# Splitting the first weight loads, moving part of a projection into the start, and reading a few short rows early, in a sliding-window attention kernel

## The chip, the cores and the metric

One core of a Trainium2 chip. The metric is the device time of one execution in microseconds (us), as the median of several executions. "Span" is the time from the first to the last instruction of the program as the profile shows it, and is shorter than the time by what lies outside it. All comparisons of times below are between executions in the fast state; one profiled execution (of e6) fell in the slow one, and is marked. A ratio is the mean time of one kernel's fast runs over that of the other's of the same rounds, so it is not quite the ratio of the medians quoted beside it. In the profile's lines `<-` before a name in brackets gives what an engine waited for, and a "trace" is the record of the one execution of a kernel that was profiled.

Engines are named as in the profile: PE does matmuls, PEld is its weight loads, DVE is VectorE, ACT ScalarE, POOL GpSimd, SP the engine that issues most loads.

## The reference

```python
# B=8, Sq=32, D=1024, Hq=32, Hkv=4, Sk=8192, Dh=128; all bfloat16
W = min(4096, max(256, Sk // 4))                       # 2048: only the last W keys and values
q = (x @ wq).reshape(B, Sq, Hq, Dh).transpose(0, 2, 1, 3)
k = jnp.repeat(k_cache[:, :, Sk - W:, :], rep, axis=1)  # rep = 8 query heads share one K/V head
v = jnp.repeat(v_cache[:, :, Sk - W:, :], rep, axis=1)
p = softmax(einsum("bhqd,bhkd->bhqk", q, k) * Dh ** -0.5)
out = einsum("bhqk,bhkd->bhqd", p, v).transpose(0, 2, 1, 3).reshape(B, Sq, Hq * Dh) @ wo
```

There are 32 pairs of a batch and a K/V head. The kernel calls each a unit; it has 2048 keys, 512 KB of K and 512 KB of V.

## The kernel before

The kernel runs the units one after another. A unit has four slots. In each slot PE makes scores for 512 keys, ACT takes their exp, and PE multiplies the exps of two slots ago with V. All other PE work (the q projection of the next group of heads, the output projection, turning K of the next unit) is hung on the slots as "pieces".

The start has no slots. It loads x and the first group's part of wq (eight chunks of 256 KB), turns x with PE, makes q of group 0, and turns K of unit 0:

```python
Q_CUT = 4
N_WARM = (7, 0, 0)

    def start(self):
        wz = self.c1.tile([P, 512], BF16, name="wz")
        nc.vector.memset(wz[:, :], 0.0)
        nc.sync.dma_start(out=x_sb[:, 0, :], in_=xf[0:P, :])
        nc.scalar.dma_start(out=x_sb[:, 1, :], in_=xf[P:2 * P, :])
        wq0 = self.load_wq(0, 0, (1, 1, 2)) + self.load_wq(0, 1, (2, 1, 1))   # chunks 0 | 1 | 2,3 | 4,5 | 6 | 7
        for p in wq0[:4]:
            p()
        self.load_k(0, 0)                    # first half of K of unit 0
        wq0[4]()
        wq0[5]()
        self.load_k(0, 1)                    # second half
        self.load_v(0, nc.sync)
        self.load_k(1)
        self.load_v(1, nc.sync)
        # ... weights of later groups are collected in self.weights
        for ui in range(2, 4):
            self.load_unit(ui)               # K and V of units 2 and 3, K of 5, two pieces of wq of group 1
        # ... memsets
        warm_up(N_WARM[0])                   # 7 matmuls of 512 columns on wz, to keep PE busy until x is there
        # ... turn x
        for c in range(self.DC):             # 8 chunks
            for h in range(self.rep):        # 8 heads
                q_mm(c, h, 0, P if c >= Q_CUT else self.NQ)      # from chunk Q_CUT on only the first 128 rows of q
            if c == self.DC - 3:
                k_turn(0); k_copy(0)         # first half of K0
        k_turn(1)                            # second half of K0
        # ... copy q of batch 0; k_copy(1); va_copy(0)
        def q_rest(k):                       # the other 128 rows, chunks Q_CUT to 7: two of these in slot 0, two in slot 1
            for h in (2 * k, 2 * k + 1):
                for c in range(Q_CUT, self.DC):
                    q_mm(c, h, P, self.NQ)
            q_copy("v", k, 1, self.B)
```

All loads but one go through SP's queue, in program order. The order after the start is set by these lines:

```python
V_T = {5: (2, (5, 6, 8, 10), 10, 17, 12), **{u: (u - 4, ...) for u in (8, 11, ...)}}  # K of these units is turned by DVE and GpSimd
W_AT = (3, 3, 4, 4, 8, 8, ...)               # after which unit's loads each piece of wq or wo is loaded

    def load_unit(self, ui):
        # K, V of the unit, then K of a V_T unit that is due, then weight pieces with W_AT == ui
    def k_pieces(self, ui):                  # PE turns K of unit 1 to 4, in the four slots of the unit before (unit 1: in the last two)
    Q_SLOTS = {1: (17, 31), ...}             # q of group 1 is made in slots 17 to 30
```

## Time and profile before

| | |
|---|---|
| time, median of 3 runs | 186.94 us (186.40 to 186.98); of 6 runs 186.74 |
| span of the profiled execution | 184.6 us |
| PE busy | 97% |
| first exp starts | 14.02 us |

These lines are from the page of the kernel before. After the span comes the busy time of each engine; then, in 40 slices of the span, the busy tenths of PE and what the DMA engines moved; the count of instruction fetches in part 3; and the shares of the chain of work that ended last.

```profile
span 184.6 us, 5089 instructions
...
PE 179.9 (97%) x2072; PEld 153.7 (83%) x2072; DVE 115.2 (62%) x267; ACT 131.8 (71%) x133; POOL 94.7 (51%) x150
...
GB/s 159 297 396 408 402 398 396 238 206 228 384 361 255 369 274 314 403 267 221 354 341 246 358 391 235 281 278 384 258 314 399 233 264 321 188 240 28 4 30 91
...
q8 instruction: 16, 0.26, 0.6%
...
PE 93%; DMA 4%; SPq 1%; DVE 1%; issue 0%
```

The table of waits, PE's lines only: who waited for whom, total us, times, the longest.

```profile
PE warm_ps L347 <- DVE wz L316: 1.2, 1, 1.2
...
PEld L377 <- DMA wq_sb<-in_wq_dram: 1.2, 2, 1.0
PEld L356 <- DMA x_sb<-in_x_dram: 0.8, 1, 0.8
PE q_ps L377 <- DMA wq_sb<-in_wq_dram: 0.7, 1, 0.7
...
PEld L370 <- DMA k_raw<-in_k_cache_dram: 0.2, 1, 0.2
```

PE waits for weights of q (L377), for x, and a little for K0's second half (L370).

The chain that ended last, in order of time, its first 18 us (start, us, what; short pieces are left out):

```profile
2.12 6.54 DMA wq_sb<-in_wq_dram
...
8.70 2.81 PE q_ps L377 x32
...
12.92 0.62 PE kf_ps L370 x8
13.54 0.44 PE s_ps L469 x4
13.98 0.89 PE q_ps L377 x16
```

Chunks 2 and 3 arrive as one load at 8.65 us; PE had finished chunk 1 at about 7.8. At 12.92 it starts to turn K0's second half, makes the first scores, and then the second half of the q matmuls (L377 x16 is 0.89 us) inside slot 0.

### The profile page before, as it was taken

To read this page: it belongs to the slowest core of one execution; us is meant where nothing else is said; L and a number is where in the kernel's file an instruction comes from. 1 tells how busy PE (TensorE), PEld (TensorE's weight loads), DVE (VectorE), ACT (ScalarE), POOL (GpSimd) and SP (SyncE) were. 2 spreads that over 40 slices of the span, in tenths; PEclk is the share of its full clock that TensorE was granted. 3 is DMA by queue.
4 is the path that set the end of the run, shared out by engine and by line. 5 is a ranking of instruction groups with operands and counts; after the bars stand their busy time and mean duration, and the time that the engine had idled before them with its cause. 6 is when DMAs were issued, how large, how long until landed. Compare 5 with 4: busy or idle time off the path is not lost.

```text
span 184.6 us, 5089 instructions
## 1 busy us (share of the span) xinstructions
PE 179.9 (97%) x2072; PEld 153.7 (83%) x2072; DVE 115.2 (62%) x267; ACT 131.8 (71%) x133; POOL 94.7 (51%) x150
## 2 busy tenths in 40 slices
PE   7899999999999999999999999999999999999994
PEld 2799999999999999987788899988787888888843
DVE  0238799994586686586467648656755865265363
ACT  2207899787789777777878677887877888888800
POOL 2000007949939959928954990797199379700000
PEclk9999999999999999999999999999999999999999
DMA  6999999999999989999999999999999999891003
GB/s 159 297 396 408 402 398 396 238 206 228 384 361 255 369 274 314 403 267 221 354 341 246 358 391 235 281 278 384 258 314 399 233 264 321 188 240 28 4 30 91
DMA packets 53082, 51.73 MB, mean 280 GB/s; under 512 B 39744, under 2 KB 40256, under 8 KB 53056
## 3 DMA queue, kind: packets, MB, share of 16 engines
q1 hardware_dynamic: 52480, 50.90, 98.9%
q10 hardware_dynamic: 576, 0.49, 0.8%
q8 instruction: 16, 0.26, 0.6%
q14 instruction: 10, 0.08, 0.2%
HBM read 41.42 MB, written 0.52 MB: 227 GB/s over the span
## 4 chain that ended last, share of the span: by engine, by line
PE 93%; DMA 4%; SPq 1%; DVE 1%; issue 0%
PE o_ps L480 31%; PE s_ps L469 30%; PE op_ps L295 15%; PE q_ps L275 11%; DMA wq_sb<-in_wq_dram 4%; PE q_ps L377 2%; PE tp L236 2%; PE kf_ps L370 1%; SPq L164 0%; DVE kT L374 0%; SPq L321 0%; DVE o_t L305 0%; DVE QT_63 L397 0%; PE cnt_ps L534 0%
## 5 line engine op out<-in xcount | busy, mean ns | idle before, releaser
L471 ACT ACTIVATE pT<-s_ps 128x1024 bf16<-128x1024 f32 x128 | 128.9, 1025 | 33.3 <-PE s_ps L469 32.3
L261 POOL TENSOR_SCALAR kTv<-kb 32x512 bf16<-32x512 bf16 x140 | 93.7, 670 | 65.1 <-PE s_ps L469 38.6
L480 PEld LDWEIGHTS <-pT 128*128 128x128 bf16 x1024 | 68.4, 98 | 3.2
L469 PEld LDWEIGHTS <-kT 128*128 128x128 bf16 x368 | 34.7, 98 | 10.4
L295 PE MATMUL op_ps<-wo_sb,OT 128*128 128x512 bf16 (+2 forms) x144 | 36.2, 356 | 0.0
L275 PE MATMUL q_ps<-xT,wq_sb 128*128 128x256 bf16 x192 | 28.1, 273 | 0.0
L480 PE MATMUL o_ps<-va_112,pT 128*128 128x129 bf16 x352 | 27.2, 220 | 0.0
L480 PE MATMUL o_ps<-va_113,pT 128*128 128x129 bf16 x352 | 27.0, 220 | 0.0
L480 PE MATMUL o_ps<-va_114,pT 128*128 128x129 bf16 x320 | 24.7, 220 | 0.0
L251 DVE STREAM_TRANSPOSE kb<-k_raw 128x512 bf16<-128x512 bf16 x36 | 23.8, 684 | 0.0
L417 DVE RECIPROCAL RL_all<-o_ps 128x2 f32<-128x2 f32 x32 | 5.3, 164 | 27.5 <-PE o_ps L480 27.5
L422 DVE TENSOR_SCALAR o_sb<-o_ps,RL_all 128x128 bf16<-128x128 f32 x64 | 19.5, 346 | 1.1
L469 PEld LDWEIGHTS <-kTv 128*128 128x128 bf16 x144 | 13.9, 98 | 5.1
L275 PEld LDWEIGHTS <-wq_sb 128*128 128x128 bf16 x192 | 17.0, 98 | 1.2
L469 PE MATMUL s_ps<-QT_63,kT 128*128 128x256 bf16 x112 | 16.8, 273 | 0.0
L424 DVE STREAM_TRANSPOSE OT<-o_sb 128x256 bf16<-128x256 bf16 x32 | 14.2, 445 | 1.1
L469 PE MATMUL s_ps<-QT_66,kT 128*128 128x256 bf16 x96 | 14.4, 273 | 0.0
L295 PEld LDWEIGHTS <-OT 128*128 128x128 bf16 x144 | 11.4, 98 | 2.3 <-DVE OT L424 0.2
L469 PE MATMUL s_ps<-QT_65,kT 128*128 128x256 bf16 x80 | 12.0, 273 | 0.0
L469 PE MATMUL s_ps<-QT_64,kT 128*128 128x256 bf16 x80 | 12.0, 272 | 0.0
L302 DVE TENSOR_TENSOR oacc<-op_ps,oacc 128x512 f32<-128x512 f32 x8 | 5.5, 682 | 7.4 <-PE op_ps L295 7.4
L411 DVE COPY va_113<-v_sb 128x2048 bf16<-128x2048 bf16 x11 | 9.5, 860 | 0.0
(45 smaller groups left out, 105.1 us busy)
## 6 DMA issues: line engine op xcount, KB each, us to landing
v_sb<-in_v_cache_dram SPq DMA_DIRECT2D x29, 512.0 KB, 6.9
wo_sb<-in_wo_dram SPq DMA_DIRECT2D x16, 512.0 KB, 6.8
wq_sb<-in_wq_dram SPq DMA_DIRECT2D x14, 512.0 KB, 6.9
k_raw<-in_k_cache_dram SPq DMA_DIRECT2D x13, 512.0 KB, 6.3
v_sb<-in_v_cache_dram SPq DMA_DIRECT2D x6, 256.0 KB, 6.5
wq_sb<-in_wq_dram SPq DMA_DIRECT2D x4, 256.0 KB, 6.4
kT<-in_k_cache_dram SPq DMA_TRANSPOSE x36, 6.8
k_raw<-in_k_cache_dram SPq DMA_DIRECT2D x2, 256.0 KB, 7.9
```

The source lines that it names most:

```text
L251: nc.vector.transpose(out=st["kb"][:, sl, :], in_=self.k_raw[ui][:, sl, :])
L261: nc.gpsimd.tensor_scalar(out=out, in0=in_, scalar1=1.0, scalar2=1.0, op0=ALU.mult, op1=ALU.mult)
L275: nc.tensor.matmul(st["ps"][:, 0:self.NQ], lhsT=self.wq_t[g, i][:, c % (DC // 2), hl * P:(hl + 1) * P], rhs=self.xT[:, c, :], start=(c == ...
L295: nc.tensor.matmul(ps[:, 0:w], lhsT=self.OT[:, gq, c, t * P:(t + 1) * P], rhs=self.wo_t[gq][:, c, n0:n0 + w], start=(k == 0), stop=(k == 7))
L302: nc.vector.tensor_tensor(out=acc, in0=ps[:, 0:w], in1=acc, op=ALU.add)
L411: self.nc.vector.tensor_copy(out=self.va[ui % 3][:, :, 0:self.Dh], in_=self.v_sb[ui][:, :, :])
L417: nc.vector.reciprocal(out=rl[:, ui * QT_N:(ui + 1) * QT_N], in_=o_ps[:, :, Dh])
L422: nc.vector.tensor_scalar(out=o_sb[:, qt, :, :], in0=o_ps[:, qt, 0:Dh].rearrange("p (i c) -> p c i", c=4), scalar1=rl[:, ui * QT_N + qt:ui ...
L424: nc.vector.transpose(out=self.OT[:, g * QT_N:(g + 1) * QT_N, :, b * self.Sq:(b + 1) * self.Sq], in_=o_sb[:, :, :, :])
L469: nc.tensor.matmul(s_ps[:, jj, :], lhsT=self.kT[ui][:, c * CJ + jj, :], rhs=q_u, start=True, stop=True)
L471: nc.scalar.activation(out=pT[:, :, :], in_=s_ps[:, :, :], func=ACT.Exp, bias=0.0, scale=self.scale)
L480: nc.tensor.matmul(o_ps[:, qt, 0:self.VW], lhsT=pT[:, jj, qt * P:(qt + 1) * P], rhs=va[:, j, 0:self.VW], start=(j == 0 and qt == 0), stop= ...
```

## The change

The intent is to shorten the start. Chunks 2 and 3 come as two loads. Chunks 4 and 5 get all their rows at once (`Q_CUT` 6), so that less is left for slots 0 and 1. The warm-up reads a constant that exists before the start, so PE need not wait for DVE. GpSimd's queue reads 16 short rows each of wq, K and V first, to take a possible cost of first access off the big loads. The V load of unit 29 is no longer cut in two.

```diff
-Q_CUT = 4
-N_WARM = (7, 0, 0)
+Q_CUT = 6
+N_WARM = (8, 0, 0)
-V_HALVES = 29
+V_HALVES = 30
@@ start
-        wz = self.c1.tile([P, 512], BF16, name="wz")
-        nc.vector.memset(wz[:, :], 0.0)
+        one = nc.const_aps.tensor
-        wq0 = self.load_wq(0, 0, (1, 1, 2)) + self.load_wq(0, 1, (2, 1, 1))
-        for p in wq0[:4]:
+        wq0 = self.load_wq(0, 0, (1, 1, 1, 1)) + self.load_wq(0, 1, (2, 1, 1))
+        for p in wq0[:5]:
             p()
         self.load_k(0, 0)
-        wq0[4]()
         wq0[5]()
+        wq0[6]()
@@
+        first = self.c1.tile([16, 3, 32], BF16, name="first")
+        for i, src in enumerate((self.wq[0:16, 0:32], self.k_cache[0, 0, self.Sk - self.W:self.Sk - self.W + 16, 0:32],
+                                 self.v_cache[0, 0, self.Sk - self.W:self.Sk - self.W + 16, 0:32])):
+            nc.gpsimd.dma_start(out=first[:, i, :], in_=src)
@@ warm_up
-                nc.tensor.matmul(warm[:, :], lhsT=wz[:, 0:P], rhs=wz[:, :], start=True, stop=True)
+                nc.tensor.matmul(warm[:, :], lhsT=one(1.0, [P, P], BF16), rhs=one(1.0, [P, 512], BF16), start=True, stop=True)
```

## The prediction

> **What bounds it now.** The page gives PE 97% busy; the chain of waits is 93% PE, 4% DMA. Its only DMA piece is the load of wq chunks 2 and 3: issued at 2.12 us, released PE at 8.70. The table of waits gives PE four real waits: warm-up on the zeroed tile (until 1.20 us), x (0.8 us, to 4.30), wq (0.7-1.0 us, to 8.70), the second K half (0.2 us, to 12.92). From the first scores (13.38 us) to the end PE runs on its own work. So the change can win only in the first 13 us, or by emptying the slots after.
>
> **What the change does, costed.**
> 1. Loads split. x lands about 4.3, chunk 0 at 6.03, chunk 1 at 6.72, chunks 2+3 together at 8.65, 4+5 at 10.0. A chunk is 8 matmuls 0.109 us apart: 0.87 us. PE runs out near 7.83. Chunk 2 alone should land near 7.7 (half of the pair's 1.93 us), so the 0.7-1.0 us wait almost closes. The extra issue (0.47 us of SP) is hidden: the stream limits, not the issuing.
> 2. Q_CUT 4 to 6 moves 16 matmuls of 128 columns (0.055 us each, 0.88 us) from the first two score slots into the start. No work disappears; it fills point 1's hole. Slots 0 and 1 shrink from 1.33 to 0.90 us each.
> 3. Warm-up: the constant of ones is written before the start barrier, so PE starts near 0.85 instead of 1.20, eight matmuls at 0.427 us end near 4.27. That spacing is the cold clock of the Trainium skill, "TensorE: Matmul & The Clock Gate", Part 1 (half rate until about 3.4 us of activity); the trace agrees: x's transposes start 0.107 us apart until about 5.7 us, then 0.055. Starting sooner may warm PE sooner: worth 0 to 0.3 us.
> 4. Short GpSimd reads. DMA moves about 400 GB/s at 3-4 us and after 10 us, but 236-303 at 4-7 and 272-293 at 8-10, when wq and K are first read, some packets taking 0.4 to 1.15 us, not 0.084. At about 400 GB/s the loss is about 1.4 us of landing time. The first packets of x took 0.7 us too. The reads should pay such a cost early. But V's first reads show no such dip, so I give it 45%. They may also slow x.
> 5. Unit 29's V in one load: nothing.
>
> **Sum.** Without help from 4: chunks 0-3 run 6.08-9.56, wait for 4+5 (10.0), 10.05-11.79, K half 12.24, chunks 6, 7 13.12, second K half 13.57: first scores 0.2 us later, 0.88 us less afterwards: net -0.7. With help: PE never waits after 6.0, first scores at about 13.1: net -1.15; earlier warmth up to -0.4 more. All on the critical path.
>
> **Predicted: 185.9 us** (186.94 before, -0.6%), eight times in ten 185.0 to 186.9. Faster by over 2%: 3%; within 2%: 95%; slower: 2%.
>
> **Signs.** Warm-up before 0.9 us; no q matmul wait near 7.8-8.7, perhaps one at chunk 4; first scores 13.0-13.6; slots 0, 1 0.9 us apart; DMA at 4-7 and 8-10 us near 400 GB/s if 4 works, unchanged if not; unit 1 on unchanged.
>
> **What would make it wrong.** x landing later because the short reads stall the engines; identity late behind the short reads; DVE copies of q becoming a wait in slots 2 and 3 (they follow V's landing, 14.15 us); the gain lost to ScalarE (1.02 us per slot against 0.90).

## More of the kernel before

PE is the bound: it is busy nearly always and the last-ending chain is 93% PE. But slices 3 to 7 (9 to 32 us, 4.6 us each) move about 400 GB/s without a break; no later stretch of that length moves as much (one single slice has 403).

## The result, and the profile after

The changed kernel takes 186.70 us (median of 6 runs, 186.08 to 187.09) against 186.74 before (6 runs). The ratio is 0.9996, with a 95% interval of 0.9972 to 1.0021: the same. The predicted gain of 0.6% is not there. 186.70 lies inside the predicted range of 185.0 to 186.9 all the same, but so does the 186.74 of the unchanged kernel: that the time fell in the range says nothing for the mechanism.

The answering lines of the page:

```profile
span 184.5 us, 5062 instructions
...
PE 180.8 (98%) x2057; PEld 154.1 (83%) x2057; DVE 115.6 (63%) x266; ACT 131.6 (71%) x133; POOL 96.3 (52%) x153
...
GB/s 155 341 369 414 405 401 391 223 184 360 283 346 257 357 243 357 401 269 241 370 361 246 364 392 233 242 327 384 261 362 345 227 260 287 216 219 0 0 33 88
...
q8 instruction: 15, 0.25, 0.5%
...
PE 83%; DMA 14%; SPq 1%; issue 0%; DVE 0%
```

The span is the same to 0.1 us, with 15 fewer matmuls. But the share of DMA in the chain went from 4% to 14%. The chain in order of time shows where:

```profile
2.59 5.97 DMA wq_sb<-in_wq_dram
...
8.58 9.36 DMA v_sb<-in_v_cache_dram
...
17.96 10.40 DMA k_raw<-in_k_cache_dram
```

The chain no longer follows PE through the first units. It follows loads up to 17.96 + 10.40 = 28.36 us, when K of unit 4 lands. Before that moment nothing that PE saved counts. The waits agree:

```profile
PEld L359 <- DMA x_sb<-in_x_dram: 0.9, 1, 0.9
PE warm_ps L350 <- PEq L645: 0.8, 1, 0.8
PEld L236 <- DMA k_raw<-in_k_cache_dram: 0.5, 2, 0.3
...
PEld L380 <- DMA wq_sb<-in_wq_dram: 0.2, 1, 0.2
...
PEld L373 <- DMA k_raw<-in_k_cache_dram: 0.2, 1, 0.2
```

The wait for chunks 2 and 3 is gone, as intended; the 0.2 us left on a load of wq (L380) is for chunks 4 and 5, which landed at 9.86 us. In its place PE waits twice for K of a later unit (L236, the turning of K). Here is the first of the two places, before and after, in PE's weight loads in order of time; and below it the second.

Before:

```profile
19.55 0.27 PEld L236 LDWEIGHTS <-k_raw 128*128 128x128 bf16 x4
...
28.45 0.27 PEld L236 LDWEIGHTS <-k_raw 128*128 128x128 bf16 x4
```

After:

```profile
19.26 0.23 PEld L236 LDWEIGHTS <-k_raw 128*128 128x128 bf16 x4 [0.26 <-DMA k_raw<-in_k_cache_dram]
...
28.41 0.23 PEld L236 LDWEIGHTS <-k_raw 128*128 128x128 bf16 x4 [0.24 <-DMA k_raw<-in_k_cache_dram]
```

The trace's issue and semaphore records give the landings. "Lead" is how much earlier an exp starts than the same exp of the kernel before.

| | K0, second half | first exp | K2 lands | K4 lands | lead at exp 4 | at exp 5 | at exp 13 | at the last exp |
|---|---|---|---|---|---|---|---|---|
| before | 12.88 | 14.02 | 19.29 | 28.40 | | | | |
| after | 13.13 | 14.27 | 19.22 | 28.37 | 0.58 | 0.32 | 0.08 | 0.09 |

The start won 0.58 us, and two waits took 0.26 and 0.24 of it. The sums close. Before, PE turned K2 0.26 us after it had landed (19.55 less 19.29); K2 now lands 0.07 us earlier; so PE can lead there by 0.33 at most, and 0.32 is measured. For K4 it is 0.05 + 0.03 = 0.08, and 0.08 to 0.09 is measured. Put shortly: the lead can be no more than 19.55 less the landing of K2, and then no more than 28.45 less the landing of K4.

How the 0.58 came about is seen in ACT's exps in order of time (start, busy us), before:

```profile
14.02 1.02 ACT L471 ACTIVATE pT<-s_ps 128x1024 bf16<-128x1024 f32 x1 [1.00 <-PE s_ps L469]
15.35 1.02 ACT L471 ACTIVATE pT<-s_ps 128x1024 bf16<-128x1024 f32 x1 [0.31 <-PE s_ps L469]
16.68 1.02 ACT L471 ACTIVATE pT<-s_ps 128x1024 bf16<-128x1024 f32 x1 [0.31 <-PE s_ps L469]
18.01 1.02 ACT L471 ACTIVATE pT<-s_ps 128x1024 bf16<-128x1024 f32 x1 [0.31 <-PE s_ps L469]
```

and after:

```profile
14.27 2.88 ACT L474 ACTIVATE pT<-s_ps 128x1024 bf16<-128x1024 f32 x3 [0.96 <-PE s_ps L472]
17.43 1.02 ACT L474 ACTIVATE pT<-s_ps 128x1024 bf16<-128x1024 f32 x1 [0.28 <-PE s_ps L472]
18.77 1.02 ACT L474 ACTIVATE pT<-s_ps 128x1024 bf16<-128x1024 f32 x1 [0.31 <-PE s_ps L472]
20.20 1.02 ACT L474 ACTIVATE pT<-s_ps 128x1024 bf16<-128x1024 f32 x1 [0.41 <-PE s_ps L472]
```

Exps are counted from 0. Exp 0 is 0.25 us later (14.27 against 14.02). Exps 0 to 2 then follow almost without a gap instead of every 1.33 us, so exp 3 (17.43 against 18.01) and exp 4 (18.77 against 19.35) are 0.58 us ahead. The last line shows the lead being lost: from exp 4 to exp 5 (18.77 to 20.20) it takes 1.43 us, where the kernel before took 1.18 (19.35 to 20.53).

Last, the stretches of the start for the kernel before. Columns: the stretch, its length, busy us of PE, PEld, DVE, ACT, POOL (with instructions), granted clock, DMA share, GB/s.

```profile
4.00:8.00 4.00, 3.97 (x33) 2.98 (x32) 0.92 (x3) 1.17 (x2) 0.00 (x0) 1.00 0.98 299
8.00:10.00 2.00, 1.30 (x12) 1.18 (x13) 0.00 (x0) 0.00 (x0) 0.00 (x0) 1.00 1.01 283
10.00:12.00 2.00, 2.00 (x34) 1.94 (x33) 0.01 (x1) 0.00 (x0) 0.00 (x0) 1.00 1.05 406
12.00:16.00 4.00, 3.95 (x64) 3.66 (x62) 3.55 (x8) 2.10 (x4) 0.00 (x0) 1.00 1.03 415
```

and after:

```profile
4.00:8.00 4.00, 4.00 (x33) 3.33 (x33) 0.92 (x3) 1.17 (x2) 0.00 (x0) 1.00 0.92 300
8.00:10.00 2.00, 2.00 (x20) 1.62 (x18) 0.00 (x0) 0.00 (x0) 0.00 (x0) 1.00 1.04 384
10.00:12.00 2.00, 2.00 (x23) 1.82 (x22) 0.00 (x0) 0.00 (x0) 0.00 (x0) 1.00 1.01 313
12.00:16.00 4.00, 3.99 (x59) 3.66 (x57) 3.29 (x7) 2.16 (x4) 0.00 (x0) 1.00 1.03 417
```

The dip at 8 to 10 us moved to 10 to 12; it did not go. By 13 us the loads are where they were, or 0.25 us behind.

### The profile page after: what moved, and what is told of

Read it like the earlier page. It is cut to its first block, busy times and chain, and to the rows that moved or that the text cites. A ratio compares the mean times of both kernels' runs of the same rounds, so it can differ in the third digit from the quotient of the medians.

```text
span 184.5 us, 5062 instructions
## 1 busy us (share of the span) xinstructions
PE 180.8 (98%) x2057; PEld 154.1 (83%) x2057; DVE 115.6 (63%) x266; ACT 131.6 (71%) x133; POOL 96.3 (52%) x153
## 4 chain that ended last, share of the span: by engine, by line
PE 83%; DMA 14%; SPq 1%; issue 0%; DVE 0%
PE o_ps L483 29%; PE s_ps L472 27%; PE op_ps L295 15%; PE q_ps L275 11%; DMA k_raw<-in_k_cache_dram 6%; DMA v_sb<-in_v_cache_dram 5%; DMA wq_sb<-in_wq_dram 3%; SPq L164 1%; PE tp L236 1%; SPq L320 0%; DVE o_t L305 0%; PE cnt_ps L537 0%
```

## The experiments

Theory A: from about 9 to 33 us the loads run at their full rate, 1.28 us for 512 KB, and K2 and K4 landed just in time before. A start that is faster on PE meets loads that are not faster, and hands the lead back. Theory B, a rival: the lead went with the phase of PE's clock. In the trace's records of the granted clock, full speed came at 5.69 us before and 6.57 us after (PE's transposes of x start 0.107 us apart until 5.6 us before and 0.055 apart from 5.7; the clock column of the stretches above shows 1.00 throughout and is no guide here). Before, PE's hole near 8 us may have hidden such a delay. Rival C: the order of the loads alone matters, not the start. A last question was whether the short reads do anything.

Twelve kernels were run, all correct, each in five timed rounds and a profile. The table has what the traces and rounds gave; the texts after it say what each was for. "Over" counts executions whose time exceeds their span by more than 2.0 us.

| kernel | Q_CUT | K0's second half lands | full clock from | lead at exp 4 | at exp 16 | at the last | ratio to before (95%) | mean span, it / before | over |
|---|---|---|---|---|---|---|---|---|---|
| changed | 6 | 13.13 | 6.57 | 0.58 | 0.09 | 0.09 | 0.9996 (0.9972 to 1.0021) | 184.58 / - | 2 of 6 |
| e1_k4_first | 6 | 13.05 | 5.26 | 0.65 | 0.57 | -0.01 | 1.0039 (1.0001 to 1.0077) | 185.00 / 184.67 | 3 of 6 |
| e2_k2_k4_first | 6 | 12.87 | 6.23 | 0.83 | 0.83 | 0.65 | 0.9994 (0.9975 to 1.0013) | 184.48 / 184.67 | 1 of 6 |
| e3_before_k2_k4 | 4 | 13.16 | 7.16 | -0.28 | -0.28 | -0.28 | 1.0034 (1.0001 to 1.0066) | 185.25 / 184.67 | 0 of 6 |
| e5_before_k4_late | 4 | 13.19 | 4.66 | -0.32 | -1.29 | -1.29 | 1.0054 (1.0032 to 1.0076) | 185.70 / 184.67 | 0 of 6 |
| e6_deadline_order | 6 | 14.10 | 3.92 | -0.39 | -0.39 | -0.68 | 1.0019 (0.9986 to 1.0051) | 184.92 / 184.65 | 1 of 6 |
| e7_before_deadline | 4 | 13.40 | 5.16 | -0.52 | -0.52 | -0.81 | 1.0022 (1.0006 to 1.0038) | 185.15 / 184.65 | 0 of 6 |
| e8_deadline_no_reads | 6 | 12.90 | 4.48 | 0.80 | 0.81 | 0.51 | 1.0006 (0.9987 to 1.0025) | 184.60 / 184.65 | 1 of 6 |
| e9_deadline_qcut4 | 4 | 12.97 | 3.86 | -0.09 | -0.09 | -0.39 | 1.0018 (1.0005 to 1.0032) | 185.05 / 184.65 | 0 of 6 |
| e10_deadline_fixed | 6 | 12.98 | 6.10 | 0.71 | 0.71 | 0.30 | 1.0025 (0.9993 to 1.0056) | 184.42 / 184.55 | 3 of 6 |
| e11_fixed_no_reads | 6 | 13.10 | 3.49 | 0.61 | 0.61 | 0.61 | 0.9979 (0.9957 to 1.0002) | 183.87 / 184.55 | 2 of 6 |
| e12_fixed_before_qcut6 | 6 | 12.45 | 6.13 | 0.97 | 0.97 | 0.97 | 1.0019 (0.9982 to 1.0056) | 184.40 / 184.55 | 3 of 6 |
| e4_no_reads | 6 | 12.89 | 4.70 | 0.82 | 0.49 | 0.49 | 1.0014 (0.9984 to 1.0043) | 184.22 / 184.55 | 5 of 6 |

Leads are of the one profiled execution, measured against the one profiled execution of the kernel before; spans are means of six executions each (five of e6, its profiled one slow) against ten or eleven of the kernel before on the same chip. One execution of the kernel before took 381 us and is left out. "Over" counts all six of e6.

### K4 ahead of the weights

```diff
-W_AT = (3, 3, 4, 4, ...)
+W_AT = (4, 4, 4, 4, ...)        # on the changed kernel: two pieces of wq of group 1 after K4 and V4
```

> The changed kernel with one more edit: the first two pieces of wq for group 1 are loaded after K and V of unit 4 instead of before them. In the trace of the changed kernel PE's lead over the kernel before (read at the exps) was 0.58 us at the fourth exp, fell to 0.32 us when PE waited for K of unit 2 (landing 19.22 us), and to 0.09 us at exp 13, where it waited for K of unit 4 (28.37 us). Theory A (the lead is handed back because K lands no earlier): the second wait goes, K of unit 4 lands near 25.7 us, the lead stays at about 0.3 us to the end, time about -0.3 us against before. Theory B (the lead is lost to the phase of PE's clock: the full clock came at 6.57 us here against 5.69 us): the order of these loads is of no account, the lead at exp 13 and later depends on the clock alone, time about the same as before (-0.1 us or less).

K4 landed at 25.35 us instead of 28.37, and the step at exp 13 went: the lead at exp 16 was 0.57; the cap set by K2, which landed at 18.98 us, is 19.55 less 18.98. Theory B alone would not have that step go with the order of the loads; but full clock came early here (5.26 us), so this run does not refute it. e2, e10 and e12, with full clock at 6.10 to 6.23 us, later than before, and the lead kept past exp 16, do. But the lead was then lost at exp 18, where q of group 1 begins and its weights, now later in the queue, landed at 33.15 and 34.46 us. These two waits, from the table of waits between 33 and 36 us, are new:

```profile
PEld L275 <- DMA wq_sb<-in_wq_dram: 0.7, 1, 0.7
PE q_ps L275 <- DMA wq_sb<-in_wq_dram: 0.4, 1, 0.4
```

The time rose a little (1.0039) instead of falling by 0.3 us: a miss in the number. The wait had moved, not gone: another sign that the queue has hardly any slack up to 34 us.

### K2 and K4 ahead

```diff
+        self.load_k(2)               # before V of unit 1; left out of load_unit(2); and W_AT as above
         self.load_v(1, nc.sync)
```

> The changed kernel with both K loads pulled ahead: K of unit 2 before V of unit 1, and K of unit 4 before the first wq pieces of group 1. Theory A: neither wait is left, the lead of about 0.6 us (or more, where the clock comes early) that the start wins stays to the last exp, time -0.5 to -0.8 us against before, 0.4 us or more better than the changed kernel was. It could be clipped a little at 33 us, where the q matmuls of group 1 start, for their weights now land as late as the second half did. Theory B: as the changed kernel, 0 to -0.1 us unless the clock comes early.

Both steps went in the profiled execution: 0.83 at exps 4 and 16, 0.65 after a small wait for the last piece of weights, and the span was 184.0. The timed executions show less: mean span 0.19 us below before, ratio 0.9994. This is below the expected 0.5 to 0.8, and asked for an order with more slack.

### The same order on the kernel before

The edit is that of e2, on the kernel before.

> The kernel before with the same two orders of loads and nothing else. Theory A: no gain by itself, 0.0 us within 0.15, since K of unit 2 (landed 19.29, wanted 19.60) and K of unit 4 (landed 28.40, wanted about 28.4) were just in time for a PE that starts its scores at 13.38 us. A rival C, that the load order alone is worth what e2 gains and the new start nothing, expects -0.4 us or more here too.

No gain, so rival C falls. The profiled execution was 0.28 us late from the first exp on, because K0's second half landed 0.28 us later, and stayed so. Two of the six executions had spans of 185.9 and 186.4; the other four had 184.7 to 184.9. What made the two long is open.

### K4 made later

```diff
-W_AT = (3, 3, 4, 4, ...)
+W_AT = (3, 3, 3, 4, ...)        # on the kernel before: one more 512 KB piece ahead of K4
```

> The kernel before with one more wq piece (512 KB) ahead of K of unit 4. One such piece takes 1.28 us of the stream. Theory A: K of unit 4 lands near 29.7 us, PE waits for it about 1.2 us near 28.4 us, and the time rises by 1.0 to 1.3 us, since nothing later gives it back. Theory B, or slack in that stage: no change beyond 0.2 us.

K4 landed at 29.74 us. PE's weight loads for it, in order of time:

```profile
29.78 0.23 PEld L236 LDWEIGHTS <-k_raw 128*128 128x128 bf16 x4 [0.97 <-DMA k_raw<-in_k_cache_dram]
```

The exps fell back by 0.97 us there (from -0.32 to -1.29) and never recovered; the mean span rose by 1.03 us. So K4's landing does set the time of the kernel before, with hardly any slack (0.05 us in its trace), as theory A has it. The trace of the kernel before shows no wait at that place: a load that is just in time looks like a load with time to spare.

### All early loads in the order of their use

```diff
-        self.load_k(1)
-        self.load_v(1, nc.sync)
-        for ui in range(2, 4):
-            self.load_unit(ui)
+        for k, u in (("k", 1), ("k", 2), ("v", 1), ("k", 5), ("k", 3), ("v", 2), ("k", 4), ("v", 3),
+                     ("w", 0), ("w", 1), ("w", 2), ("v", 4), ("w", 3)):
+            ...                          # load that K, V or piece of wq of group 1
@@ V_T
+       8: (4, range(18, 22), 21, 28, 16),      # turning of K8 two slots later than before
@@ run
-        loads = {8: [4, 5, 6, 7], ...}
+        loads = {8: [5, 6, 7], ...}             # and K8 first
```

> The changed kernel with all loads of the first 34 us in the order in which they are wanted: K1, K2, V1, K5, K3, V2, K4, V3, three wq pieces of group 1, V4, the fourth piece, then K8 (whose turning on VectorE starts two slots later). In the run with K2 and K4 alone ahead, the lead was 0.83 us at exp 4, 0.67 us after exp 18 (a wait for the last wq piece, landing 33.78 us), and the time did not show it (0.9994), while its profiled execution did (span 184.0 against 184.6). With 1.28 us per 512 KB, K2 should land near 18.0, K4 24.5, the last wq piece 32.4, each about a microsecond ahead of need. Theory A: no wait of PE for DMA between exp 0 and the end; the lead of exp 4 (0.5 to 0.9 us) is there at the last exp; mean span of the timed executions 0.5 to 0.9 us below that of the kernel before. Rival: the start's lead is itself not there in most executions (the profiled ones were lucky); then the mean span stays within 0.25 us of before.

Inconclusive by itself. In the profiled execution chunk 2 landed only at 8.69 us and K0's second half at 14.10, 1.22 us later than before, and the first exp came 1.23 us later. The emptied slots brought this down to 0.39 us, and no K2 or K4 wait followed; but then all four kernels of this set lost 0.29 us at exp 32. The waits of e8 name the reason, my own edit to K8, which made PE wait for GpSimd's share of the turning:

```profile
PEld L475 <- POOL kTv L262: 0.3, 1, 0.3
```

Its span of 187.2 us has a second reason outside the argument: the last two stores of the output took 3.7 and 3.4 us to land instead of 1.5.

### The same on the kernel before

The edit is that of e6, on the kernel before.

> The kernel before with the same order of loads in the deadline order. Theory A: within 0.2 us of the kernel before, since its PE waited for no load after 13 us. If it gains 0.4 us or more, the order is worth something by itself, for instance because executions other than the profiled one do wait for loads at units 2 and 4.

It lost: mean span 0.50 us longer. Of this 0.29 is the K8 edit; the rest goes with K0's second half, which in the profiled execution landed 0.52 us later. The expected 0.2 was missed on account of the K8 edit, but the order alone gains nothing, again against rival C.

### Without the short reads

The edit is that of e6, less the three `nc.gpsimd.dma_start` lines.

> The deadline-order version of the changed kernel without the three short reads on GpSimd's queue. In the trace of the changed kernel they were issued at 1.29 to 2.84 us but landed at 5.8 to 7.8 us, after the first wq chunk (5.64 us), and the later loads landed no earlier (second K half 13.13 us against 12.88). If they do nothing: same time as the version with them within 0.2 us, chunks land as before. If they help: 0.3 us or more slower, and the stretch of 4 to 10 us moves less.

K0's second half landed at 12.90, as early as with the reads or earlier, and the mean span was 0.32 us shorter than e6's. So the reads did not help here. That difference rests on one execution of e6 with a span of 186.4 us; without it e6's mean is 184.55.

### With Q_CUT back at 4

The edit is that of e6, with `Q_CUT = 4`.

> The deadline-order version of the changed kernel with the cut of q back at chunk 4, so that the second halves of chunks 4 and 5 are again done in the first two score slots. Theory A with the sums of the prediction: first scores about 0.2 to 0.3 us earlier than with the cut at 6 only if PE was not waiting for the chunks there, and 0.88 us of matmuls back in slots 0 and 1: the lead at exp 4 falls from 0.5-0.9 to about 0 to 0.3 us, time 0.4 to 0.7 us longer than the version with the cut at 6.

K0's second half landed within 0.1 us of the kernel before, and the lead at exp 4 was -0.09. With `Q_CUT` 6, e8 and e2 landed that half within 0.03 us of before, and led by 0.80 and 0.83. In all nine traces with `Q_CUT` 6 the lead grows by 0.83 to 0.84 us from exp 0 to exp 4, in the four changed orders with `Q_CUT` 4 by nothing. So the whole lead of the change is the emptied slots 0 and 1: about 0.84 us, less what the first exp comes later. The mean span tells less: it is 0.13 us longer than that of e6, which differs by `Q_CUT` alone, against an expected 0.4 to 0.7; without e6's one execution of 186.4 it would be 0.50.

### The order of use, with K8 put back

The edit is that of e6 without the `V_T` line.

> The changed kernel with the deadline order of loads, and the turning of K8 put back on its old slots. The earlier version had put it two slots later, and all four kernels with it lost 0.29 us at exp 32, where PE waited for GpSimd's share of that turning. Theory A: that step is gone, the lead at exp 4 stands to the last exp. In ten traces the first exp starts 1.14 us (0.01 either way) after K0's second half has landed, so the lead at exp 4 should be 0.84 us less the amount by which that landing is later than 12.88 us: 0.5 to 0.8 us when it lands at 12.9 to 13.2. Mean span of the timed executions 0.4 to 0.8 us below before. Rival (the lead is taken by something still later): the lead falls again after exp 32.

The step at exp 32 is gone, and 0.71 us of lead stood up to exp 64. Then PE stopped for 0.4 us, from 102.2 to 102.6 us. No other trace has it. From the table of waits between 90 and 108 us:

```profile
DVE va L418 <- DMA v_sb<-in_v_cache_dram: 2.0, 2, 1.1
...
PEld L275 <- issue: 0.4, 1, 0.4
PE q_ps L275 <- DVE QT L278: 0.3, 1, 0.3
```

The first line of PE names no releaser, the second does, and both are the same stop. A load of V landed at 100.07 us, DVE had waited 1.06 us for it, and its copy of q (L278), in line behind, ended only at 102.55; PE's next q matmul waited for that copy and started at 102.60. So 0.41 us of this lead went to a late load too, by way of DVE. In the kernel before that V (of unit 17) landed at 96.94 us, 2.28 us before its copy; why it came so late here is open. The mean span is 0.13 us below before; the expected 0.4 to 0.8 was missed.

### The same without the short reads

> The same without GpSimd's three short reads. If the reads do nothing: mean span within 0.2 us of the version with them, K0's second half at about 12.9 to 13.2 us in both. If they help, 0.3 us or more longer; if they cost, 0.2 us or more shorter.

This is the best version: median 185.94 against 186.42 us, ratio 0.9979 (0.9957 to 1.0002), mean span 0.68 us below before, and all six spans between 183.6 and 184.2. The interval just touches 1, so a faster time is likely rather than shown. PE's weight loads for K2 and K4 in order of time:

```profile
18.93 0.27 PEld L236 LDWEIGHTS <-k_raw 128*128 128x128 bf16 x4
...
27.84 0.27 PEld L236 LDWEIGHTS <-k_raw 128*128 128x128 bf16 x4
```

No wait stands beside them, where the changed kernel waited 0.26 and 0.24 us. The chain of its page is PE again:

```profile
PE 95%; DMA 3%; DVE 1%; SPq 0%; issue 0%
```

The 0.61 us of lead at exp 4 is there at the last exp.

### Only Q_CUT 6 on the kernel before, in the order of use

The edit is the loads of e10 and `Q_CUT = 6` on the kernel before; chunks 2 and 3 stay one load.

> The kernel before with the deadline order of loads and the cut of q at 6, and nothing else of the change: chunks 2 and 3 still come in one load, the warm-up is the old one, no short reads. If the emptied score slots alone make the lead, it is 0.84 us less the delay of the first exp. With chunks 2 and 3 landing together at 8.65 us or so, PE has four chunks of 0.87 us to do from there, then two K halves and the last two chunks: the first exp should come 0.3 to 0.6 us later than 1.14 us after K0's second half, so the lead at exp 4 is 0.2 to 0.5 us, and the split of the load is worth the rest. If the split is worth nothing the first exp stays at 1.14 us after that landing.

K0's second half landed at 12.45, the earliest of all, for no reason of the edit. The first exp came 1.44 us after it, where in the other 13 traces it came 1.14 to 1.16 us after it. By the expectation these 0.30 us would be the worth of the split. The trace does not allow that: PE reached K0's second half without a wait, and no later than with the split.

```profile
12.69 0.54 PEld L374 LDWEIGHTS <-k_raw 128*128 128x128 bf16 x8
```

PE's last q matmul before that half starts at 12.69 us here, and at 12.66 to 13.02 in seven of the eight traces with the split and `Q_CUT` 6 (13.91 in e6). So PE was as early without the split; the half was merely earlier still. Chunks 2 and 3 together landed at 7.86 us, not at 8.65. An estimate from this trace: from the start of chunk 2 (7.90) to K0's second half (12.80) PE needs 4.90 us, so with the pair at 8.65 it would get there near 13.6, where the changed kernel was there at 13.17. The split may thus be worth something once `Q_CUT` is 6; no run shows how much. The lead of 0.97 held to the end.

### The changed kernel without the short reads

> The changed kernel as it was, loads in the old order, without GpSimd's three short reads. Theory A: the time is set by K2 and K4 of the stream, whatever the start does: same as the kernel before and the changed kernel within 0.2 us, with waits of PE at K2 and K4, unless the first exp comes late. If the reads help by landing the stream earlier, K4 lands later than 28.4 us here and the time is 0.3 us or more longer.

With the old order the steps are back: 0.82 at exp 4, 0.67 at exp 5, 0.49 at exp 13. They are smaller, for K2 and K4 happened to land at 18.87 and 27.96; the caps of the changed kernel hold here too (19.55 less 18.87 is 0.68, 28.45 less 27.96 is 0.49). The mean span is 0.33 us below before, more than the 0.2 expected, but the ratio is 1.0014. The reason is in the last column of the table: five of six executions had 2.4 to 2.7 us outside the span, where the kernel before never had more than 1.9.

### What lies outside the span

That column sorts the kernels. With `Q_CUT` 4 (e3, e5, e7, e9: 24 executions, and 32 of the kernel before) none is over 2.0 us. With `Q_CUT` 6 it is 21 of 54. In the changed kernel it is two of six, with 2.6 and 2.7 us outside; its mean is 2.05 us against 1.79 for those 32 executions. So in its time 0.26 us went there, beside what the waits took. The page's count of 16 KB instruction fetches goes with it. In the five profiled executions with 2.5 us or more outside (the changed kernel, e1, e2, e4, e12) the page counts 15 fetches in the span, and the sixteenth packet starts 1.7 to 1.9 us after the last instruction (186.3 us in the changed kernel). In the other nine it counts 16 and 1.7 to 1.9 us lie outside. The traces with `Q_CUT` 6 have about 30 instructions of PE fewer, and the last fetch comes later in them: at 174 us before, at 180 to 186 with `Q_CUT` 6. That the shorter program makes it late, and that the late fetch causes the extra time, is inferred from this match; no run forced it, and the count alone does not decide it, for e10 and the changed kernel have the same count and fetch at 180 and 186 us.

## Why the prediction was right and wrong

The time fell in the range, and that is luck of a range that reached up to the unchanged kernel's time. The gain did not come.

- **Point 1, the split: right in size, wrong in worth.** Chunk 2 landed at 7.48 us (7.7 predicted) and the wait at 8.7 us went; 0.2 us of wait for chunks 4 and 5 came at 9.9. But the hole near 8 us was not what held the first scores. In 13 of 14 traces the first exp starts 1.14 to 1.16 us after K0's second half lands, over landings from 12.87 to 14.10 us. What the split is worth through the work it makes room for is not shown (e12).
- **Point 2, the moved matmuls: right.** Slots 0 and 1 shrank; the lead is 0.83 us less the delay of the first exp (0.88 predicted).
- **Point 3, the warm-up: right as a fact, of no effect.** PE started at 0.79 us, and the half-rate start that the Trainium skill describes ("TensorE: Matmul & The Clock Gate", Part 1) is there: full clock came between 3.49 and 7.16 us over the 14 traces, 2.7 to 6.0 us after PE's first matmul, where the prediction took about 3.4. Yet the first exp follows K0's landing by the same 1.14 us whichever it was. This is also where theory B falls.
- **Point 4, the short reads: the 55% case.** They landed at 5.81, 7.18 and 7.75 us, the first of them after the first chunk of wq itself (5.64). They came too late to pay anything in advance. Without them (e11 against e10, e8 against e6, e4 against the changed kernel, the last pair from different rounds) the mean spans were 0.3 to 0.6 us shorter, but the ratios do not all follow: 1.0014 in e4 against 0.9996 with the reads. A cost of the reads is possible but not shown: the intervals overlap in all three pairs.
- **The sum: its first part right, its last step wrong.** "First scores 0.2 us later, 0.88 us less afterwards: net -0.7" was 0.25, 0.83 and 0.58. The step that failed is "**From the first scores (13.38 us) to the end PE runs on its own work**", and with it "**All on the critical path**". It was read from a table without waits. K2 had 0.26 us to spare, K4 0.05, and behind them a queue of loads at its full rate. In place of it, the runs show the lead capped at 0.33 and then 0.08 us (changed kernel); PE held up by 0.97 us when K4 is made later (e5); and the lead kept to the end when K2, K4 and the weights of group 1 come in the order of use (e11, e12).
- **Not seen at all:** the 0.3 to 1.2 us more outside the span in 21 of 54 executions with `Q_CUT` 6 (2.1 to 3.0 us against 1.8), which go with an instruction fetch after the span in the five of them that have a trace.

What stays open: what makes the loads dip between 4 and 12 us, to 249 GB/s in the lowest stretch of 2 us, at other places in each execution; what the split is worth; why V of unit 17 came late in e10; the time outside the span; the long spans in two executions of e3. And the leads are each read from one profiled execution: in the times no order of loads is faster than the kernel before beyond doubt.

## What to carry to other kernels

A table of waits tells where an engine is late, not where it is just in time. Before counting on a gain upstream, take for each later load the time of use less the time of landing; here the smallest of these was all of the gain that could pass, and if the loads run at full rate, it must be made larger by their order first. When work is moved, also look at what lies outside the span: the time that counts includes it.

## What the Trainium skill lacked or had wrong

- "Runtime: NRT & Kernel Launch", section "Instruction fetch mechanics", says that an engine refills its program in 16 KiB blocks and that crossing a block costs "one DMA tail-bump, mostly hidden". The blocks are there (16 of 16 KB on the page). Whether crossing one is always hidden stays open: in 13 of 14 traces the landings of 512 KB loads, mostly 1.28 us apart, show a gap of 2.1 to 2.8 us at the time of the first such packet (in the kernel before from 16.71 to 19.29 us, with the packet at 16.83, 1.11 us long). That gap is part of why K2 was only just in time. That the packet makes it is not shown: e6 has the packet (16.63 us) and no gap, the second packet (23.5 to 24.9 us) has no such gap in any trace, and through the gap of the kernel before the loads moved 389 to 418 GB/s.
- No page tells of a fetch after the program's last instruction. In five traces here it goes with 2.5 to 2.8 us outside the span instead of 1.7 to 1.9.
- "DMA: Bandwidth & Descriptors", section "Anatomy of one DMA — SWDGE (gpsimd) path", gives a fixed cost of about 2.0 us for a DMA of GpSimd's queue. Three such DMAs of 1 KB, issued beside full queues, took 4.5 to 4.9 us from issue to landing in the changed kernel (1.29 to 5.81, 2.33 to 7.18, 2.84 to 7.75 us).
- The same page gives rates for a steady stream; none tells of the first microseconds, where this core's loads ran at 291 to 360 GB/s from 4 to 8 us and at 415 to 421 from 12 to 16 us over the 14 traces.
